# A Fourier-mixing and mixture-of-experts kernel on one core: the first expert layer of 512-row blocks in seven block products

## Chip, core and metric

The kernel runs on one core of one Trainium2 chip. The metric is the device time of one launch in microseconds (us); a time of the kernel before is the median of three launches. Profiles and traces are of one launch each, taken by the hardware profiler. The engines are called as the profile calls them: PE is TensorE (matmuls), PEld its weight loads, DVE is VectorE, ACT is ScalarE, POOL is GpSimd, SP is SyncE, which here issues most transfers.

## What is computed

The input is 8 batches of 2496 rows of 256 numbers. Each batch goes through a two-dimensional Fourier transform of which the real part is kept. Each of the 19,968 rows that result goes to the one of 8 experts whose gate value is the largest, and an expert is a network of two layers with 1024 numbers between them.

```python
X = np.fft.fft(np.fft.fft(x, axis=1), axis=2).real     # (8, 2496, 256)
x = X.reshape(19968, 256)
logits = x @ w_gate                                    # 8 experts
expert_idx = np.argmax(logits, axis=1)
gate_w = softmax(logits)[row, expert_idx]
for e in range(8):                                     # the rows of expert e
    h = np.maximum(x[rows_of_e] @ w1[e], 0.0)          # first layer, 256 to 1024
    y[rows_of_e] = h @ w2[e]                           # second layer, 1024 to 256
return gate_w[:, None] * y
```

All data are fp32. In the profile one fp32 matmul of the program shows as two MATMUL records and two LDWEIGHTS records; in the kernel it is one call of `mm`.

## The kernel before

The kernel works in rounds. While the rows of one batch go through the experts, the transform of the next batches is computed beside them. Rows are written by expert into `Xs` in device memory and come back as blocks of 512, 256 or 128 rows of one expert. The plan of the rounds is fixed: round 0 has two blocks of 256 rows and four of 128, round 1 four of 256, round 2 three of 512, rounds 3 to 6 five of 512 each, round 7 five of 512, then seven of 256 mixed with 21 of 128. That makes 28 blocks of 512 rows, 13 of 256 and 25 of 128.

The banks of PSUM, the memory that matmuls write, are shared out like this (a tile fills one of the eight banks or part of one):

```python
pm_ = ctx.enter_context(tc.tile_pool(name="pm_", bufs=3, space=PSUM))   # transform and routing
pst = ctx.enter_context(tc.tile_pool(name="pst", bufs=1, space=PSUM))   # transposes of a block
psh = ctx.enter_context(tc.tile_pool(name="psh", bufs=2, space=PSUM))   # first layer
psy = ctx.enter_context(tc.tile_pool(name="psy", bufs=2, space=PSUM))   # second layer
```

A block is transposed by `turn`, while the second layer of the block ahead of it runs:

```python
def turn(size, xb):
    xT = bp.tile([128, 2, BIG], F32, tag="xT", name="xT", bufs=1)
    n = min(size // 128, 2)
    for h in range(-(-size // 256)):
        pt = pst.tile([128, 2, n, 128], F32, tag="t", name="pt")
        for c in range(2):
            for t in range(n):
                nc.tensor.transpose(pt[:, c, t], xb[:, 2 * h + t, c * 128:(c + 1) * 128], ident[:])
        vec.tensor_scalar(xT[...], pt[...], con["alt"][:], None, op0=ALU.mult)
        yield xT
```

`experts` is a generator. Each `yield` of a number above zero says how much expert work was just issued, and gives the main loop the chance to issue steps of the transform before the next piece. With 512 rows `m` is 1, `FC` is 8 and `n` is 4, so that a block yields 8 times 1 and 4 times 2, 16 in all:

```python
for k, (b, size, last, at) in enumerate(todo):
    n, m = size // 128, BIG // size
    ...
    for f in range(FC // m):                                   # first layer
        ph = psh.tile([128, m, size], F32, tag="h", name="ph")
        for j in range(m):
            for c in range(2):
                mm(ph[:, j], w1_sb[:, c, (m*f+j)*128:(m*f+j+1)*128], xT[:, c, 0:size], c == 0, c == 1)
        o = hT[:, m * f:m * (f + 1), 0:size]
        if f % 2:
            vec.tensor_scalar(o, ph[:], 0.0, None, op0=ALU.max)
        else:
            act.activation(o, ph[:], ACTF.Relu)
        yield 1
    ...                                                        # turned = turn(the next block)
    for i in range(n):                                         # second layer
        xT = next(turned, xT)
        py = psy.tile([128, D], F32, tag="y", name="py")
        for f in range(FC):
            mm(py[:], hT[:, f, i * 128:(i + 1) * 128], w2_sb[:, f], f == 0, f == FC - 1)
        act.activation(y[:, i], py[:], ACTF.Copy, scale=xb[:, i, D + 1:D + 2])
        put_row(out, ro[:, i:i + 1], y[:, i], NT - 1, "out")   # indirect DMA, issued by POOL
        yield 2
```

The main loop spreads some 44 steps (`TICKS`) of the transform over the first 70% of a round's expert work; `side` is the generator of these steps:

```python
total = 16 * sum(k * size for size, k, _ in rounds()[b - 1]) / BIG
while done < total:
    w = next(work)
    done += w
    due += TICKS * w / (0.7 * total) if w else 1
    while due >= 1:
        next(side, None)
        due -= 1
for _ in side:
    pass
```

A step of the second stage of the transform holds, on PE, two matmuls of 120 columns into a tile `p` (copied by ACT to `zz`) and two of 145 and 146 columns into another `p`; from that ACT copies `zs` and DVE makes `lg` and two halves of `rows`. With every second such step goes a step of the first stage of the batch after: DVE folds `xq` (additions of 104 x 1024 and 104 x 508), PE makes two matmuls of 256 columns into `s`, ACT copies them to `t`. The steps of `route` are chains of small DVE operations up to `oh`, on which the matmuls into `rk` wait, and indirect writes of rows to `Xs` by POOL. All PSUM tiles of these steps come from the three buffers of `pm_`.

Of the kernel before, what the change touches and what calls it, by code (L numbers as in the profile page):

```python
# [34 lines left out]
E, F = 8, 1024  # L35
# [134 lines left out]


TICKS = 44
WARM = 16
MOST = max(k for now in rounds() for _, k, _ in now)

# [16 lines left out]
def kernel(ctx: ExitStack, tc, x, w_gate, w1, w2, out):  # L192
# [3 lines left out]
    def mm(o, lhsT, rhs, start=True, stop=True, **kw):  # L196
        nc.tensor.matmul(o, lhsT=lhsT, rhs=rhs, start=start, stop=stop, **kw)  # L197
# [305 lines left out]
    def turn(size, xb):  # L503

        xT = bp.tile([128, 2, BIG], F32, tag="xT", name="xT", bufs=1)
        n = min(size // 128, 2)
        for h in range(-(-size // 256)):
            pt = pst.tile([128, 2, n, 128], F32, tag="t", name="pt")
            for c in range(2):
                for t in range(n):  # L510
                    nc.tensor.transpose(pt[:, c, t], xb[:, 2 * h + t, c * 128:(c + 1) * 128], ident[:])  # L511
            vec.tensor_scalar(xT[:, :, 256 * h:256 * h + 128 * n], pt[:].rearrange("p c t k -> p c (t k)"),  # L512
                              con["alt"][:], None, op0=ALU.mult)
            yield xT

    def experts(todo):

        got, xT = [], None  # L520

        def fetch_some(k, most=3):

            while k + len(got) < len(todo) and len(got) < most and todo[k + len(got)][:3] in tabs:
                b, size, last, at = todo[k + len(got)]
                got.append(fetch(b, size, tabs[b, size, last], at))

        for k, (b, size, last, at) in enumerate(todo):
            n, m = size // 128, BIG // size
            if not k:  # L530
# [5 lines left out]
                for xT in turn(size, got[0][0]):  # L536
                    pass
            fetch_some(k)
            xb, w1_sb, w2_sb = got.pop(0)
            turned = iter(())  # L540
            follow = todo[k + 1] if k + 1 < len(todo) else None
            ro = bp.tile([128, BIG // 128], I32, tag="ro", name="ro", bufs=4)
            vec.tensor_copy(ro[:, 0:n], xb[:, 0:n, D])
            hT = bp.tile([128, FC, BIG], F32, tag="hT", name="hT", bufs=1)
            for f in range(FC // m):
                ph = psh.tile([128, m, size], F32, tag="h", name="ph")
                for j in range(m):
                    for c in range(2):
                        mm(ph[:, j], w1_sb[:, c, (m * f + j) * 128:(m * f + j + 1) * 128], xT[:, c, 0:size],
                           c == 0, c == 1)  # L550
# [6 lines that stand above are left out]
            if follow:  # L557
                while follow[:3] not in tabs:
                    yield 0
                fetch_some(k + 1, 2)  # L560
                turned = turn(follow[1], got[0][0])
# [61 lines left out]
    for _ in range(WARM):  # L623
        pw = psy.tile([128, D], F32, tag="y", name="py")
# [35 lines left out]
    for b in range(1, B):  # L660
# [66 lines left out]
```

## Time and profile before

| | before |
|---|---|
| three launches | 1398.54, 1403.64, 1409.75 us |
| profiled launch: span | 1367.9 us |
| PE busy | 1323.7 us, 97% of the span |
| PEld busy | 1007.3 us, 74% |
| DVE, ACT, POOL busy | 381.1, 284.2, 325.8 us |
| first layer, PE busy (tile `ph`) | 585.4 us, of it 396.7 us in the 512-column form |
| second layer, PE busy (tile `py`) | 580.8 us |
| granted TensorE clock, mean | 0.984 of full speed |

The span of the profiled launch is some 36 us less than the median of the three launches. The table of groups gives, for each kind of instruction, the sum of busy time, the mean duration of one, and after the second bar the idle time of its engine just before it with what ended that idle time. The records of matmuls overlap, so a mean duration times a count is more than the busy time; the pace of PE is read from the start times in the timeline.

### The profile page before, as it was taken

The numbers are of one execution on the slowest core, as the hardware profiler recorded it, in microseconds if no ns is written. First come the engines' busy times: TensorE is split into PE (matmuls) and PEld (weight loads), VectorE is DVE, ScalarE is ACT, GpSimd is POOL, SyncE is SP. The second block draws the span as 40 slices with busy tenths as digits, with TensorE's granted clock in tenths as the row PEclk, the third lists the DMA queues.
The fourth block names the chain that finished last, engine by engine and source line by source line (L and its number), as shares of the span: only waits on it lengthen the run. The fifth ranks groups of instructions, "written<-read, shape, count | busy, mean of one in ns | idle before, by whom it ended". The sixth has DMA issues, their size and how long they took to land.

```text
span 1367.9 us, 17145 instructions
## 1 busy us (share of the span) xinstructions
PE 1323.7 (97%) x6190; PEld 1007.3 (74%) x6190; DVE 381.1 (28%) x1182; ACT 284.2 (21%) x656; POOL 325.8 (24%) x335
## 2 busy tenths in 40 slices
PE   5769999999999999999999999999999999999998
PEld 3659987776766667767767767666776689999997
DVE  4643334431333224222233212224111111111111
ACT  1422131321222113211222112221111111111111
POOL 0335144143032211331122411331311111111111
PEclk8779999999999999999999999999999999999999
DMA  8769876455364424534234242414323327777772
GB/s 251 248 243 344 325 242 243 160 161 203 132 203 159 182 106 143 159 137 171 95 138 169 92 156 99 173 65 173 127 97 120 131 92 273 278 283 282 275 264 102
DMA packets 63089, 249.50 MB, mean 182 GB/s; under 512 B 10057, under 2 KB 24883, under 8 KB 43420
## 3 DMA queue, kind: packets, MB, share of 16 engines
q1 hardware_dynamic: 46231, 203.33, 42.0%
q0 software_dynamic: 15888, 42.14, 8.5%
q10 hardware_dynamic: 885, 2.94, 0.6%
q8 instruction: 49, 0.80, 0.2%
q14 instruction: 36, 0.29, 0.1%
HBM read 194.97 MB, written 54.83 MB: 183 GB/s over the span
## 4 chain that ended last, share of the span: by engine, by line
PE 53%; issue 31%; POOL 7%; DMA 2%; DVE 1%; POOLq 0%; ACT 0%; SPq 0%; ACTq 0%; DVEq 0%
PE py L197 23%; PE ph L197 22%; POOL out_dram L212 5%; PE p L197 4%; PE s L197 2%; POOL Xs L212 2%; PE pt L511 2%; DMA Xs<-rows,pi 1%; DMA xb<-Xs 1%; DMA Xs<-pad,ti 0%; DMA w_sb<-in_moe_w_dram 0%; POOLq L212 0%; PE rk L197 0%; DVE hT L553 0%; DVE rows L389 0%
## 5 line engine op out<-in xcount | busy, mean ns | idle before, releaser
L197 PE MATMUL ph<-xT,w_sb 128*128 128x512 f32 (+2 forms) x2112 | 585.4, 431 | 1.9 <-DMA w_sb<-in_moe_w_dram 1.9
L197 PE MATMUL py<-w_sb,hT 128*128 128x256 f32 x2608 | 580.8, 379 | 0.0
L197 PEld LDWEIGHTS py<-w_sb,hT 128*128 128x128 f32 x2608 | 487.3, 190 | 62.0
L197 PEld LDWEIGHTS ph<-xT,w_sb 128*128 128x128 f32 x2112 | 339.7, 191 | 196.5 <-issue 177.4
L212 POOL DMA_INDIRECT out_dram<-y,ro x163 | 159.1, 976 | 864.8 <-ACT y L568 846.5
L553 DVE TENSOR_SCALAR hT<-ph 128x512 f32<-128x512 f32 x163 | 112.7, 692 | 688.8 <-PE ph L197 344.7
L568 ACT ACTIVATE y<-py,xb 128x256 f32<-128x256 f32 x163 | 77.3, 474 | 602.6 <-PE py L197 602.6
L212 POOL DMA_INDIRECT Xs<-rows,pi x160 | 158.7, 992 | 172.0 <-issue 73.3
L555 ACT ACTIVATE hT<-ph 128x512 f32<-128x512 f32 x163 | 97.3, 597 | 326.8 <-PE ph L197 326.8
L512 DVE TENSOR_SCALAR xT<-pt,table 128x512 f32<-128x512 f32 (+1 forms) x94 | 63.3, 674 | 71.0 <-PE pt L511 71.0
L197 PE MATMUL s<-xq,w 104*112 104x256 f32 (+2 forms) x208 | 59.5, 409 | 12.8 <-DVE xq L276 12.6
L197 PEld LDWEIGHTS p<-table,t 120*128 120x128 f32 x352 | 54.7, 204 | 18.5 <-issue 12.0
L387 DVE COPY lg<-p 128x16 f32<-128x16 f32 x80 | 13.9, 174 | 181.6 <-ACT zs L384 181.4
L511 PE MATMUL pt<-table,xb 128*128 128x128 f32 x326 | 51.9, 275 | 8.7 <-DMA xb<-Xs 8.7
L511 PEld LDWEIGHTS pt<-table,xb 128*128 128x128 f32 x326 | 40.5, 142 | 25.3 <-issue 11.6
L197 PE MATMUL p<-table,t 120*128 120x120 f32 (+1 forms) x352 | 57.0, 289 | 1.7 <-DVE rows L389 1.4
L197 PE MATMUL p<-table,zz 128*128 128x145 f32 (+1 forms) x320 | 56.2, 300 | 2.6 <-DVE rows L389 1.4
L197 PEld LDWEIGHTS s<-xq,w 104*112 104x112 f32 x208 | 38.3, 198 | 25.0 <-DVE xq L276 9.3
L197 PEld LDWEIGHTS p<-table,zz 128*128 128x128 f32 x320 | 45.9, 196 | 6.2 <-issue 2.4
L389 DVE SCALAR_TENSOR_TENSOR rows<-p,zs 128x129 f32<-128x129 f32 x160 | 48.2, 343 | 1.4 <-issue 0.2
L300 ACT COPY t<-s 112x512 f32<-112x512 f32 x48 | 27.9, 584 | 52.2 <-PE s L197 43.6
L358 ACT COPY zz<-p 128x240 f32<-128x240 f32 (+1 forms) x88 | 31.0, 352 | 35.0 <-PE p L197 34.6
(81 smaller groups left out, 303.2 us busy)
## 6 DMA issues: line engine op xcount, KB each, us to landing
w_sb<-in_moe_w_dram SPq DMA_DIRECT2D x132, 1024.0 KB, 7.4
xq<-in_x_dram SPq DMA_DIRECT2D x24, 896.0 KB, 9.7
xb<-Xs SPq DMA_DIRECT2D x28, 516.0 KB, 3.8
Td<-t SPq DMA_DIRECT2D x18, 448.0 KB, 3.3
t<-Td SPq DMA_DIRECT2D x8, 768.0 KB, 5.4
t<-Td SPq DMA_DIRECT2D x8, 640.0 KB, 6.4
xb<-Xs SPq DMA_DIRECT2D x13, 258.0 KB, 3.2
xb<-Xs SPq DMA_DIRECT2D x25, 129.0 KB, 2.5
```

The source lines that it names most:

```text
L197: nc.tensor.matmul(o, lhsT=lhsT, rhs=rhs, start=start, stop=stop, **kw)
L212: return unordered(pool.indirect_dma_start(out=dst, out_offset=bass.IndirectOffsetOnAxis(ap=idx, axis=0), in_=rows, in_offset=None, bounds ...
L300: act.copy(t1[:, 2 * half:2 * half + 2], ps[:])
L358: act.copy(zz[:, :, g * GP:g * GP + n], p2[:])
L387: vec.tensor_copy(lg[:, k:k + 2], p3[:, NY:NY + 2 * E].rearrange("p (m e) -> p m e", m=2))
L389: vec.scalar_tensor_tensor(rows[:, k + m, 0:NY], p3[:, 0:NY], zs[:, 0:1], zs[:, 1:], op0=ALU.add, op1=op)
L511: nc.tensor.transpose(pt[:, c, t], xb[:, 2 * h + t, c * 128:(c + 1) * 128], ident[:])
L512: vec.tensor_scalar(xT[:, :, 256 * h:256 * h + 128 * n], pt[:].rearrange("p c t k -> p c (t k)"), con["alt"][:], None, op0=ALU.mult)
L553: vec.tensor_scalar(o, ph[:], 0.0, None, op0=ALU.max)
L555: act.activation(o, ph[:], ACTF.Relu)
L568: act.activation(y[:, i], py[:], ACTF.Copy, scale=xb[:, i, D + 1:D + 2])
```

## The change

The aim is to spend fewer matmul columns on the first layer of the 28 blocks of 512 rows. A product of two matrices that are each cut into two by two parts takes eight products of parts when done plainly. It can be done with seven, with some sums and differences of parts ahead of the products and others behind them (the form of Strassen and Winograd). Here w1 of an expert is cut into two halves of its 256 inputs (`c`) and two halves of its 1024 outputs, the rows of a block into two halves of 256.

- `left`, four additions or subtractions of 128 x 512 on POOL, makes the combinations of the parts of w1; three go to a new buffer `ws`, one back into `w1_sb`.
- `right`, four of 128 x 256 on DVE, does the same for the parts of the transposed block; three go to `xs`, one back into `xT`. Both belong to `turn` now, so they are issued beside the second layer of the block ahead.
- `seven` does the products, with a moving operand of 256 columns instead of 512, in two groups of seven. They go to five PSUM banks, `a` to `e`; a bank is reused in the group as soon as its first content was read. DVE and ACT add up the parts and apply the ReLU on the way to `hT`.
- The four pools `pst`, `psh` and `psy` become one pool `pse` of these five banks, of which the transposes use `e`, the plain first layer `a` and `c`, the second layer `b` and `d`. `pm_` keeps its three.
- `seven` has no `yield`: no step of the transform is issued within the first layer of such a block. The second layer yields twice per 128 rows instead of once, so the sum per block stays 16. The 0.7 of the main loop becomes 0.6.

Blocks of 256 and 128 rows keep the plain first layer.

```diff
+HALVED = (512,)
...
-    pst = ctx.enter_context(tc.tile_pool(name="pst", bufs=1, space=PSUM))
-    psh = ctx.enter_context(tc.tile_pool(name="psh", bufs=2, space=PSUM))
-    psy = ctx.enter_context(tc.tile_pool(name="psy", bufs=2, space=PSUM))
+    pse = ctx.enter_context(tc.tile_pool(name="pse", bufs=1, space=PSUM))
...
+    def left(eng, o, a11, a12, a21, a22):
+        eng.tensor_tensor(o[0], a21, a22, op=add)
+        eng.tensor_tensor(o[1], o[0], a11, op=sub)
+        eng.tensor_tensor(a21, a11, a21, op=sub)
+        eng.tensor_tensor(o[2], a12, o[1], op=sub)
+        return a11, a12, o[2], a22, o[0], o[1], a21
...                                      # right: four of the same kind on b11, b12, b21, b22
     def turn(size, got):
+        if size in HALVED:
+            ws = bp.tile([128, 3, F // 2], F32, tag="ws", name="ws", bufs=1)
+            f = F // 2
+            l = left(pool, [ws[:, k] for k in range(3)],
+                     *(w1_sb[:, c, k * f:(k + 1) * f] for k in range(2) for c in range(2)))
...                                      # transposes and xT as before, pt in bank "e"
+        if size in HALVED:
+            th = size // 2
+            xs = bp.tile([128, 3, th], F32, tag="xs", name="xs", bufs=1)
+            r = right(vec, [xs[:, k] for k in range(3)],
+                      *(xT[:, c, k * th:(k + 1) * th] for c in range(2) for k in range(2)))
+            yield l, r
+    def seven(size, l, r, hT):
+        th = size // 2
+        fp = 512 // th
+        half = FC // 2
+        def product(g, k, o, fresh=True):
+            for j in range(fp):
+                f = g * fp + j
+                mm(o[:, j], l[k][:, f * 128:(f + 1) * 128], r[k], fresh and not j, j == fp - 1, skip_group_check=True)
+        for g in range(half // fp):
+            a, b, c, d, e = (pse.tile([128, fp, th], F32, tag=k, name=k) for k in "abcde")
...                                      # p1, u2, u3 in SBUF; h11 to h22 are parts of hT
+            product(g, 0, a)
+            act.copy(p1[:], a[:])
+            product(g, 5, b)
+            vec.tensor_tensor(u2[:], p1[:], b[:], op=add)
+            product(g, 6, d)
+            vec.tensor_tensor(u3[:], u2[:], d[:], op=add)
+            product(g, 4, c)
+            vec.tensor_tensor(h22, u3[:], c[:], op=add)
+            product(g, 1, a, False)
+            act.activation(h11, a[:], ACTF.Relu)
+            act.activation(h22, h22, ACTF.Relu)
+            product(g, 3, e)
+            vec.tensor_tensor(h21, u3[:], e[:], op=add)
+            act.activation(h21, h21, ACTF.Relu)
+            product(g, 2, c, False)
+            vec.tensor_tensor(h12, u2[:], c[:], op=add)
+            act.activation(h12, h12, ACTF.Relu)
...
-            for f in range(FC // m):
-                ph = psh.tile([128, m, size], F32, tag="h", name="ph")
+            if size in HALVED:
+                seven(size, *xT, hT)
+            for f in range(FC // m if size not in HALVED else 0):
+                ph = pse.tile([128, m, size], F32, tag="ac"[f % 2], name="ph")
...
-                py = psy.tile([128, D], F32, tag="y", name="py")
+                py = pse.tile([128, D], F32, tag="bd"[i % 2], name="py")
                 for f in range(FC):
                     mm(py[:], hT[:, f, i * 128:(i + 1) * 128], w2_sb[:, f], f == 0, f == FC - 1)
+                    if f == FC // 2 - 1 and size in HALVED:
+                        yield 2
...
-            due += TICKS * w / (0.7 * total) if w else 1
+            due += TICKS * w / (0.6 * total) if w else 1
```

More of the change, by code (lines that the diff above doesn't have):

```diff
@@ L501, in fetch, with right, turn @@
         return xb, w1_sb, w2_sb
-    def turn(size, xb):
+    add, sub = ALU.add, ALU.subtract
+    def left(eng, o, a11, a12, a21, a22):
[4 more added lines that the diff above has]
+        return a11, a12, o[2], a22, o[0], o[1], a21
+    def right(eng, o, b11, b12, b21, b22):
+        eng.tensor_tensor(o[0], b12, b11, op=sub)
+        eng.tensor_tensor(o[1], b22, o[0], op=sub)
+        eng.tensor_tensor(b12, b22, b12, op=sub)
+        eng.tensor_tensor(o[2], b21, o[1], op=sub)
+        return b11, b21, b22, o[2], o[0], o[1], b12
+    def turn(size, got):
+        xb, w1_sb, _ = got
         xT = bp.tile([128, 2, BIG], F32, tag="xT", name="xT", bufs=1)
         n = min(size // 128, 2)
+        if size in HALVED:
[3 more added lines that the diff above has]
+                     *(w1_sb[:, c, k * f:(k + 1) * f] for k in range(2) for c in range(2)))
         for h in range(-(-size // 256)):
-            pt = pst.tile([128, 2, n, 128], F32, tag="t", name="pt")
+            pt = pse.tile([128, 2, n, 128], F32, tag="e", name="pt")
             for c in range(2):
@@ L514, in turn @@
             yield xT
+        if size in HALVED:
[14 more added lines that the diff above has]
+            a, b, c, d, e = (pse.tile([128, fp, th], F32, tag=k, name=k) for k in "abcde")
+            p1, u2, u3 = (bp.tile([128, fp, th], F32, tag=n, name=n, bufs=1) for n in ("p1", "u2", "u3"))
+            h11, h12, h21, h22 = (hT[:, k * half + g * fp:k * half + (g + 1) * fp, t * th:(t + 1) * th]
+                                  for k in range(2) for t in range(2))
+            product(g, 0, a)
[15 more added lines that the diff above has]
+            act.activation(h12, h12, ACTF.Relu)
     def experts(todo):
@@ L535, in experts @@
                     yield 0
-                for xT in turn(size, got[0][0]):
+                for xT in turn(size, got[0]):
                     pass
@@ L560, in experts @@
                 fetch_some(k + 1, 2)
-                turned = turn(follow[1], got[0][0])
+                turned = turn(follow[1], got[0])
             y = bp.tile([128, BIG // 128, D], F32, tag="y", name="y", bufs=3)
@@ L622 @@
     nc.sync.dma_start(out=wg[:], in_=w_gate)
-    for _ in range(WARM):
-        pw = psy.tile([128, D], F32, tag="y", name="py")
+    for k in range(WARM):
+        pw = pse.tile([128, D], F32, tag="bd"[k % 2], name="py")
         mm(pw[:], ones[:], bc(ones[:], 1, 2))
```

## The prediction, made before the changed kernel ran

> **What bounds the kernel now.** I read the page's busy shares and slices first, then the groups by form, the waits of PE, the timeline of PE where no step of the transform is left, and busy time by round.
>
> ```profile
> PE 1323.7 (97%) x6190; PEld 1007.3 (74%) x6190; DVE 381.1 (28%) x1182; ACT 284.2 (21%) x656; POOL 325.8 (24%) x335
> ...
> PE   5769999999999999999999999999999999999998
> ```
>
> PE is busy 97% of the span, and all that it lacks lies in the first three slices (some 100 us of start-up). No other engine passes 28%. Busy time alone does not prove that PE is at its limit, so the pace comes from the start times of a run of pure expert blocks:
>
> ```profile
> 998.68 13.90 PE L197 MATMUL ph<-xT,w_sb 128*128 128x512 f32 x32
> 1012.41 0.60 PE L511 MATMUL pt<-table,xb 128*128 128x128 f32 x4
> 1012.85 3.62 PE L197 MATMUL py<-w_sb,hT 128*128 128x256 f32 x16
> 1016.31 0.60 PE L511 MATMUL pt<-table,xb 128*128 128x128 f32 x4
> 1016.75 10.53 PE L197 MATMUL py<-w_sb,hT 128*128 128x256 f32 x48
> 1027.11 13.90 PE L197 MATMUL ph<-xT,w_sb 128*128 128x512 f32 x32
> ```
>
> Columns: start, length, what. One block takes 1027.11 - 998.68 = 28.43 us. The first layer is 1012.41 - 998.68 = 13.73 us for 16 fp32 matmuls of 512 columns: 0.858 us each, 1.676 ns per column. The second is 10.36 us (1016.75 to 1027.11) for 24 matmuls of 256 columns: 0.4317 us each, 1.686 ns per column. So half as many columns per weight load costs only 0.6% more per column. Nothing stands between the groups: this is PE's own pace.
>
> Beside the transform it is the same:
>
> ```profile
> 385.36:544.45 159.09, 159.09 (x661) 110.81 (x661) 45.38 (x135) 34.83 (x81) 39.00 (x40) 1.00 0.43 151
> 544.45:703.54 159.09, 159.09 (x661) 110.81 (x661) 45.39 (x135) 34.76 (x81) 39.01 (x40) 1.00 0.42 145
> ```
>
> Two rounds of five blocks (columns: stretch, length, then busy us of PE, PEld, DVE, ACT, POOL; last granted clock, DMA share, GB/s). Five pure blocks would be 142.15 us, which leaves 16.9 us for a round's steps. Their PE work, counted from the kernel, is some 2560 columns of 120 or 80, 2910 of 145 and 146, and 3328 of the first stage: 8800 x 1.68 = 14.8 us, with 1 to 2 us of small matmuls. So the steps wait for practically nothing. The few waits of PE in the whole launch:
>
> ```profile
> PE s L197 <- DVE xq L276: 12.6, 3, 5.1
> PE pt L511 <- DMA xb<-Xs: 8.7, 3, 7.0
> PE pr L197 <- DMA t<-Td: 5.0, 2, 3.8
> PE rk L197 <- DVE oh L410: 4.9, 4, 2.6
> ```
>
> (us in total, times, longest; most of it at the start.) Conclusion: columns of PE set the time; what takes columns away is gained, unless it makes PE wait.
>
> **What the Trainium skill says.** "TensorE: Matmul & The Clock Gate", Part 2, step-by-step: weight loads are pulled ahead of running matmuls and overlap them. The trace agrees: the loads of `py` take 190 ns each, the matmuls of `py` follow each other every 216 ns (half of 0.4317 us) with 0.0 us idle. "GPSIMD Engine Reference", 3.1: a two-input elementwise operation costs about 2.6 cycles per element there, 4497 ns measured for 2048 fp32 elements; a quarter of it, 1.1 us for 128 x 512, is my estimate for one operation of `left`. No run here has one yet. "SBUF — State Buffer", Who interferes with whom: a DVE instruction with two SBUF inputs and a GpSimd instruction that reads SBUF exclude each other for the whole instruction. That would bear on `left` against the folds of the transform and `right`; the trace of before has no elementwise work on POOL and cannot show it.
>
> **The change, part by part.**
>
> 1. First layer of a 512-row block. Away: 16 matmuls of 512 columns, 13.73 us. In: 2 groups x 7 products x 2 matmuls = 28 matmuls of 256 columns, the very form of `py`: 28 x 0.4317 = 12.09 us. Saved 1.64 us per block, times 28 blocks = **46 us**, 3.4% of the profiled span.
>
> 2. Adding up inside `seven`. A product is two matmuls, 0.86 us. Per group of 6.04 us DVE has five additions of 128 x 512, from 0.69 us each by the ReLU row (692 ns for the same shape out of PSUM): 3.5 us. ACT has a copy and four ReLUs at 0.6 us (597 ns): 3.0 us. Both fit. I follow the banks from the group's start at 0: `a` is full at 0.86 and needed again at 3.45; its copy ends near 1.7. `c` is full at 3.45 and needed at 5.2; DVE has read it by about 4.3. The next group takes `a` at 6.04, read by 5.1. So each bank comes free about a microsecond early. The second layer needs the parts of the last-but-one product only at its seventh matmul, some 3 us later. Cost on PE: about 0.
>
> 3. `left`: 4 x 1.1 = 4.5 us of POOL per block (126 us in all, POOL 326 to about 450 of 1330). Its first result is needed one second layer later (over 14 us), and the weights were fetched a block earlier. Hidden, but it can hold DVE folds for up to 1 us apiece.
>
> 4. `right`: 4 x about 0.36 us of DVE (between 242 ns for 80 and 681 ns for 508 elements), issued before the third row group of the second layer, so over 6 us ahead. Hidden.
>
> 5. The steps move. In a five-block round 44 steps / (0.6 x 80) = 0.92 per unit of work, and the second layer alone carries them: 1.83 after each half row group of 4 matmuls (1.73 us). Before it was 0.79 per 1.72 us of first layer. Steps in pairs are closer to each other than their chains: PE to ACT to DVE and back over three `pm_` buffers, DVE 0.17 + 2 x 0.34 = 0.86 us per step plus folds. Rounds 0 and 1 already run 44 / (0.7 x 32) = 1.96 per unit, and there the trace shows one wait of 0.9 us and 0.3 us of smaller ones. Walking through the changed order of a five-block round I find three places: the first `pr` and `p` (0.3 us), one `s` behind `rows` (0.7 us), and the first `rk`, which comes two steps behind the last `rows` (1 to 2 us). I take **2 us per round, four rounds: 8 us**. The three-block round has 3.06 steps per half row group: **3 us**. Tighter steps in rounds 0 and 1: 1 us, against 1.6 us of a wait for `xb` (near 229 us) that an earlier end of the steps may take away. Sum: about 10 to 12 us, with the scatter of POOL against DVE in it.
>
> 6. Round 7's 28 small blocks (at half and a quarter of 28.43 us for 256 and 128 rows: 7 x 14.2 + 21 x 7.1 = some 250 us), the start and the transfers' bytes stay as they are.
>
> Net: 46 - 10 = 36 us. That is 2.6% of the profiled span; from 1403.6 us I come to **1368 us**.
>
> **Rivals.** (a) *The steps, squeezed into half the time, make PE wait.* For: every step is a chain through three engines and three buffers, and `rk` waits on a chain of seven DVE operations. Against: steps three in a row (around 175 us) cost the kernel before only some 0.4 us in waits. If it holds, 5 us per round and more: a gain of 15 to 20 us, 1385 us, within 2%. (b) *POOL or DVE becomes the bound of the first layer*: `left` much slower than estimated, or queued behind indirect writes that wait for rows. For: POOL works in order, and each `put_row` waits for another engine. Against: no steps lie in the first layer, so POOL's queue is empty when `left` starts. It would cost 2 to 5 us per block, 55 us and more, and the change would be slower: 1410 us or above. (c) *All is hidden*: 46 us and the `xb` wait, 1356 us.
>
> **Range and chances.** From all hidden (46 to 48 us, and launch-to-launch scatter of 5 us: 1351) to rival (a) at its worst (1392). Faster by over 2% needs 28 us, waits of under 18 us; I give that 0.70. Within 2%: 0.27, nearly all rival (a). Slower: 0.03, rival (b).
>
> **What the profile after would show.** Products into `a` to `e` with 28 x 0.43 us per block and blocks 26.8 us apart at the start of round 7: step 1 right. Idle of PE on DVE or ACT inside `seven`: step 2 wrong. A PE wait for POOL (`ws`), or operations of `left` above 3 us: step 3 wrong. Rounds of five blocks should fall from 159.1 to about 153 us (159.1 - 8.2 + 2); if they stay above 156, step 5 is wrong, and `rk`, `s` or `p` in PE's waits will say where. The prediction would also fail if matmuls that take turns between banks and weights keep a slower pace than `py` does.

## The result, and the profile after

| | before | after |
|---|---|---|
| median of four launches each, one session | 1401.29 us | 1467.34 us |
| ratio after/before, 95% interval | | 1.0461 [1.0412, 1.0509] |
| profiled launch: span | 1367.9 us | 1465.1 us |
| mean granted TensorE clock | 0.984 | 0.951 |

The change makes the kernel 4.6% slower; the prediction had 2.6% faster. From the page of the changed kernel, the busy shares and two rows of the slices:

```profile
PE 1332.3 (91%) x6862; PEld 1161.3 (79%) x6862; DVE 578.7 (39%) x1462; ACT 380.7 (26%) x824; POOL 477.2 (33%) x447
...
PE   5687989987998799988998989988998999999998
...
PEclk8779998999999999989999999999999999999999
```

The row of PE was nines before, from the fourth slice to the last but one; now it has sevens and eights up to the end of the transform. It has unbroken nines only in the last quarter, where no step runs beside the experts. No other engine passes 39%, so what appeared is waiting, not a new bound.

The products themselves do what they were to do. PE's timeline of the changed kernel (start, length, what) for the last block of round 6, beside which no step of the transform is left; round 7 starts at 1067.93:

```profile
1041.01 1.03 PE L198 MATMUL a<-xT,w_sb 128*128 128x256 f32 x4
1041.88 1.03 PE L198 MATMUL b<-xs,ws 128*128 128x256 f32 x4
...
1053.68 3.62 PE L198 MATMUL py<-w_sb,hT 128*128 128x256 f32 x16
...
1067.93 1.03 PE L198 MATMUL a<-xT,w_sb 128*128 128x256 f32 x4
```

From block to block 1067.93 - 1041.01 = 26.92 us, where before it was 28.43: 1.51 us saved. A product takes 1041.88 - 1041.01 = 0.87 us, and there is no gap between the fourteen.

Where the transform runs beside them it is otherwise. Three rounds of five blocks, before and then after (columns as in the prediction: stretch, length, busy us of PE, PEld, DVE, ACT, POOL, clock, DMA share, GB/s):

```profile
339.84:817.24 477.40, 477.30 (x1981) 332.51 (x1980) 136.13 (x402) 104.45 (x244) 117.00 (x120) 1.00 0.41 145
```

```profile
385.94:904.50 518.56, 475.20 (x2341) 410.38 (x2340) 250.23 (x552) 156.54 (x333) 199.45 (x180) 0.96 0.37 134
```

The ideal for a round is 159.1 less five times the expected 1.64 us, 150.9 us. The changed kernel takes 518.56 / 3 = 172.9 us. PE is idle for (518.56 - 475.20) / 3 = 14.5 us of it and busy for 158.4 us, 7.5 us more than the ideal. Of this excess, 4.8 us are the clock: it is at one half for 37.6 us of the three rounds, PE is busy for 28.5 of them, and half of that is lost. Another 0.7 us is gain that did not come (1.51 instead of 1.64 us a block); the other 2 us are not explained here. The waits of PE in the whole launch (us, times, longest):

```profile
PE c L198 <- DVE hT L571: 29.5, 7, 6.8
PE rk L198 <- DVE oh L409: 21.6, 15, 2.8
PE p L198 <- ACT zz L357: 19.7, 11, 6.2
PE p L198 <- issue: 17.9, 8, 4.0
```

The first is inside `seven`: bank `c` is to be written a second time and DVE has not read it. The other three are transform steps. Seven waits of up to 6.8 us are not what a slightly tight bank would give. The timeline of one of them, in the fourth block of round 6, PE, ACT, DVE and POOL together (in brackets: idle time before, and what ended it):

```profile
1006.29 1.03 PE L198 MATMUL a<-xT,w_sb 128*128 128x256 f32 x4
...
1008.28 0.97 POOL L213 DMA_INDIRECT Xs<-rows,pi  x1 [0.31 <-issue]
...
1009.61 0.58 ACT L565 COPY p<-a 128x512 f32<-128x512 f32 x1 [2.42 <-PE d L198]
...
1012.48 0.69 DVE L567 TENSOR_TENSOR u<-p,b 128x512 f32<-128x512 f32 x1 [11.62 <-PE e L198]
1013.39 0.97 POOL L213 DMA_INDIRECT out_dram<-y,ro  x1 [0.31 <-issue]
1015.25 0.69 DVE L569 TENSOR_TENSOR u<-u,d 128x512 f32<-128x512 f32 x1 [2.08 <-remote]
1016.68 0.69 DVE L571 TENSOR_TENSOR hT<-u,c 128x512 f32<-128x512 f32 x1 [0.75 <-remote]
...
1017.52 1.97 PE L198 MATMUL c<-xT,ws 128*128 128x256 f32 x4 [5.27 <-DVE hT L571]
```

`a` is complete at 1007.3. ACT has nothing else to do, yet its copy starts at 1009.61. DVE has been idle for 11.62 us and starts its first addition 2.3 us after that copy has ended, and the next two 2.8 and 1.4 us later, although `d` and `c` are full by 1009.9. All that while POOL issues indirect writes back to back, nine of them, 1.28 us apart, from 1003.17 to 1013.39 (two are shown, the others cut). The increments by which PE tells that it is done are recorded at 1006.69, 1009.53, 1012.39 and 1015.22, then three within 0.12 us; the starts of ACT at 1009.61 and of DVE at 1012.48 and 1015.25 follow one of these by 0.03 to 0.09 us. So the engines are not slow; **they learn late that their input is there**. I call these late signals.

After the wait comes a second cost. Two stretches of the same place, with the columns as above, show the clock at 0.50 for 3.4 us:

```profile
1006.00:1017.00 11.00, 5.90 (x27) 4.53 (x25) 1.69 (x3) 1.26 (x3) 6.53 (x7) 1.00 0.26 91
1017.60:1021.00 3.40, 3.40 (x9) 2.69 (x10) 1.05 (x2) 1.66 (x3) 0.00 (x0) 0.50 0.00 0
```

The same happens to a transform step in the second layer of the changed kernel:

```profile
454.48 0.68 PE L198 MATMUL p<-table,t 120*128 120x120 f32 x4 [0.16 <-issue]
455.38 0.97 POOL L213 DMA_INDIRECT Xs<-rows,pi  x1 [0.31 <-issue]
456.66 0.97 POOL L213 DMA_INDIRECT out_dram<-y,ro  x1 [0.30 <-issue]
457.94 0.97 POOL L213 DMA_INDIRECT Xs<-rows,pi  x1 [0.31 <-issue]
460.92 0.36 ACT L357 COPY zz<-p 128x240 f32<-128x240 f32 x1 [7.60 <-remote]
...
461.33 1.34 PE L198 MATMUL p<-table,zz 128*128 128x145 f32 x4 [6.17 <-ACT zz L357]
```

ACT idles 7.60 us; the matmuls for its copy were done 5.8 us earlier. PE waits 6.17 us and then needs 1.34 us for four records that take 0.67 at full clock.

### The profile page after: what moved, and what is told of

It reads as the page before. It is cut to its first block, busy times and chain, and to the rows that moved or that the text cites. A ratio compares the mean times of both kernels' runs of the same rounds, so it can differ in the third digit from the quotient of the medians.

```text
span 1465.1 us, 19369 instructions
## 1 busy us (share of the span) xinstructions
PE 1332.3 (91%) x6862; PEld 1161.3 (79%) x6862; DVE 578.7 (39%) x1462; ACT 380.7 (26%) x824; POOL 477.2 (33%) x447
## 4 chain that ended last, share of the span: by engine, by line
PE 60%; issue 21%; DVE 5%; POOL 4%; another core or an unknown queue 3%; ACT 1%; DMA 1%; POOLq 0%; DVEq 0%; ACTq 0%
PE py L198 25%; PE a L198 7%; PE c L198 7%; PE p L198 5%; PE b L198 3%; PE d L198 3%; PE e L198 3%; PE ph L198 3%; POOL out_dram L213 3%; PE pt L535 2%; PE s L198 2%; POOL Xs L213 1%; DMA Xs<-rows,pi 1%; DVE eq L403 1%
## 5 line engine op out<-in xcount | busy, mean ns | idle before, releaser
L213 POOL DMA_INDIRECT Xs<-rows,pi x160 | 159.0, 994 | 149.2 <-DVE rows L388 53.2
L198 PE MATMUL ph<-xT,w_sb 128*128 128x128 f32 (+1 forms) x1216 | 190.3, 313 | 2.3 <-issue 1.3
L198 PEld LDWEIGHTS ph<-xT,w_sb 128*128 128x128 f32 x1216 | 173.2, 193 | 15.8 <-issue 2.4
L621 DVE TENSOR_SCALAR hT<-ph 128x512 f32<-128x512 f32 x51 | 35.3, 691 | 288.3 <-issue 209.8
L506 POOL TENSOR_TENSOR ws<-w_sb 128x512 f32<-128x512 f32 x28 | 35.6, 1271 | 315.7 <-issue 289.9
L567 DVE TENSOR_TENSOR u<-p,b 128x512 f32<-128x512 f32 x56 | 38.5, 688 | 223.7 <-PE b L198 109.1
L198 PE MATMUL a<-xT,w_sb 128*128 128x256 f32 x448 | 121.5, 395 | 3.1 <-issue 1.8
L198 PEld LDWEIGHTS a<-xT,w_sb 128*128 128x128 f32 x448 | 87.8, 198 | 18.0 <-issue 3.4
L198 PE MATMUL c<-xT,ws 128*128 128x256 f32 x224 | 63.0, 407 | 29.5 <-DVE hT L571 29.5
L573 ACT ACTIVATE hT<-a 128x512 f32<-128x512 f32 x56 | 33.4, 597 | 176.0 <-PE a L198 135.3
L198 PEld LDWEIGHTS c<-xT,ws 128*128 128x128 f32 x224 | 44.7, 203 | 38.5 <-issue 32.1
```

The costliest lines, as they stand in the source:

```text
L213: return unordered(pool.indirect_dma_start(out=dst, out_offset=bass.IndirectOffsetOnAxis(ap=idx, axis=0), in_=rows, in_offset=None, bounds ...
L506: eng.tensor_tensor(o[0], a21, a22, op=add)
L567: vec.tensor_tensor(u2[:], p1[:], b[:], op=add)
L573: act.activation(h11, a[:], ACTF.Relu)
```

## The experiments

The theories. **S**: the steps, squeezed beside the second layer only, cost the time by their own chains. **H**: late signals cost it, and the five banks of `seven`, each used again within a few matmuls, feel them most. **L**: `left` on POOL holds up DVE. **P**: late signals belong to the changed kernel only. Each run is compared with launches of the kernel before that were made beside it on the same chip; late signals were there in most sessions and absent in one, where the kernel before takes 1371 us instead of 1391 to 1403. The profiled launch of before was one without them too.

This table shows the three five-block rounds together, one third of each sum; the excess is busy time over 150.9 us with products and over 159.1 without.

| kernel | round, us | PE idle | excess busy |
|---|---|---|---|
| before, with or without late signals | 159.1 | 0.0 | 0 |
| after | 172.9 | 14.5 | 7.5 |
| left_dve | 172.9 | 14.5 | 7.5 |
| steps (squeeze, plain first layer) | 170.1 | 6.8 | 4.1 |
| spread (products, steps spread) | 162.2 | 7.4 | 3.9 |
| d_before (fewer indirect writes) | 160.0 | 0.7 | 0.2 |
| d_after | 162.6 | 7.8 | 3.9 |
| d_spread | 160.5 | 6.4 | 3.2 |
| p_after (writes to `Xs` one at a time) | 160.6 | 6.9 | 2.8 |
| p_spread | 157.7 | 4.8 | 2.1 |
| best, late signals (r_best) | 157.1 | 4.7 | 1.6 |
| best, without (v_best) | 155.1 | 3.0 | 1.2 |

**The kernel before, once more.** No edit.

> The kernel before, run once more with a trace. In the trace of the changed kernel the semaphore increments of PE, DVE and ACT arrive up to 7 us (PE) late while POOL issues indirect writes in a row; in the first trace of before (1367.9 us) all of PE's arrive within 14 ns. Theory H, held signals (something holds back the engines' increments while POOL makes its indirect writes, in some launches, whatever the kernel): the other launches of before take about 1400 us because of it, so this trace has late increments too and a span near 1400 us. Rival P (the lateness belongs to the changed program alone): none here, and the 30 us between 1370 and 1400 us are something else.

Measured: 1392.27 us, ratio 0.9989 [0.9975, 1.0002]; profiled 1388.7 us. This launch has late signals: an eviction of `y`, which follows the last matmul of `py` by 0.04 us otherwise, comes up to 4.8 us after it. Its waits of PE:

```profile
PE s L197 <- DVE xq L276: 11.0, 3, 5.7
PE p L197 <- ACT zz L358: 10.5, 8, 3.9
```

The wait of `p` for `zz` was 0.8 us in the first launch. All that is lost lies in rounds 0 to 2, which grow by 20.8 us (339.8 to 360.6); the rounds of five stay at 159.1. P falls in part: the kernel before meets late signals too, but in this launch only in rounds 0 to 2. In the rounds of five none of the 120 evictions of `ph` starts over 0.04 us after its matmuls and its engine's work ahead of it are done, though POOL issues up to 13 indirect writes in a row there. So it does not show that the kernel before has slack for late signals; it has none to meet there. (At least 57 of PE's 909 increments have no record in this trace, some of them where the reader starts at once, so lateness is read here from the starts.) Against this launch the changed one loses 25.3 us in rounds 0 to 2, 41.2 in rounds 3 to 5, 10.4 in round 6 and gains 0.5 in round 7: together 76 us.

**Products, with the steps spread as before.** `seven` yields eight times 1, spread over its fourteen products, the second layer once per 128 rows, and 0.7 is back.

```diff
-                seven(size, *xT, hT)
+                yield from seven(size, *xT, hT)        # 8 times 1 in all
...
-                    if f == FC // 2 - 1 and size in HALVED:
-                        yield 2
...
-            due += TICKS * w / (0.6 * total) if w else 1
+            due += TICKS * w / (0.7 * total) if w else 1
```

> The changed kernel, but with the steps of the transform spread as before: the first layer yields 8 times within its 14 products, the second once per row group, and 0.7 in place of 0.6. Theory S (the squeezed steps make PE wait): the waits on oh, zz and rows go away and the time falls below before, to 1350 to 1375 us. Theory H (held signals together with the tight reuse of five banks): the waits of the products for DVE and ACT stay, since indirect writes now fall into the first layer as well; 1430 us or more.

Measured: 1408.02 us, 1.0119 [1.0083, 1.0154]. Of the loss of 4.6% in after, 1.2% is left, so the placing of the steps matters; but the products still cost 15 us where they should save 46. It is neither the 1350 to 1375 us of S alone nor the 1430 and more of H alone. Waits of PE:

```profile
PE p L198 <- ACT zz L357: 9.7, 7, 4.5
PE pt L535 <- DVE xT L536: 9.6, 7, 1.5
PE c L198 <- DVE hT L583: 8.6, 8, 3.0
PE a L198 <- ACT hT L587: 7.7, 4, 2.3
```

Banks `c` and `a` of `seven` and the transposes in `e` wait without any squeeze. S alone is not enough.

**Steps squeezed, plain first layer.** The complement: no products, no `left`, no `right`; the five banks, the 0.6 and the steps beside the second layer only stay.

```diff
-HALVED = (512,)
+HALVED = ()
+BESIDE = (512,)
...
-                yield 1
+                if size not in BESIDE:
+                    yield 1
...
-                    if f == FC // 2 - 1 and size in HALVED:
+                    if f == FC // 2 - 1 and size in BESIDE:
```

> The plain first layer of before in the changed kernel's pools (five banks), with the steps of the transform beside the second layer only and 0.6: no products, no combinations, nothing new on POOL. Theory S: this alone costs most of the 46 us saved and the 66 us lost, so 1470 us or more against 1401 of before. Theory H with tight banks: the plain first layer has 1.7 us per bank and two banks in turn, so it loses little: 1405 to 1425 us.

Measured: 1447.35 us, 1.0375 [1.0344, 1.0407]: 54 us lost without a single product. The five banks are not it: with the same plain layer in them and the steps spread over 0.7 (the nine-block run below), rounds 0 to 2 take 84.0, 82.6 and 107.4 us, in the launch of before above 82.0, 82.4 and 107.3. Waits of PE:

```profile
PE rk L199 <- DVE oh L410: 15.2, 11, 2.8
PE p L199 <- issue: 13.0, 9, 2.4
PE s L199 <- DVE xq L276: 12.4, 3, 5.2
PE p L199 <- ACT zz L358: 10.7, 8, 3.1
```

H put it at 1405 to 1425 and S at 1470 or more; it fell between, nearer to S. By round: the squeeze costs 11.0 us in each round of five, 12.6 in round 6, 13.7 in rounds 0 and 1 together (170.9 + 82.4 to 180.1 + 86.9), which hold no block of 512 rows and feel only the 0.6 and the banks (with 0.7 and the same banks, in the spread form, they end at 255.3 instead of 267.0, so it is mostly the 0.6). It costs 0.9 in round 2. The steady rounds add up: 11.0 for the squeeze, 162.2 - 150.9 = 11.3 for the products with spread steps, together 22.3, against 172.9 - 150.9 = 22.0 in the changed kernel. Two faults of like size, then, though not independent ones, as the thinned writes below show. Round 2 (107.3 us in the launch of before above) is the exception: 117.3 with products and spread steps, 119.3 after, so there the products are nearly all of the loss.

**`left` on DVE.**

```diff
-            l = left(pool, [ws[:, k] for k in range(3)],
+            l = left(vec, [ws[:, k] for k in range(3)],
```

> The changed kernel with the four combinations of w1 on DVE in place of POOL, about 4 x 0.69 us of DVE per block. Theory L (elementwise work on POOL disturbs: it shuts DVE out, which in the trace stretches an operation of 0.24 us to 1.2 to 1.3 us, and it delays POOL's writes): 1400 us or less. Theories H and S: POOL's indirect writes and the place of the steps are the same, so within 20 us of the changed kernel's 1467 us.

Measured: 1462.43 us, 1.0486 [1.0459, 1.0513]; its rounds of five are those of after. L falls as the cause. The mutual hold-up it rests on is real, as the timeline of the changed kernel shows:

```profile
480.38 0.22 DVE L402 TENSOR_REDUCE mx<-lg 128x10 f32<-128x80 f32 x1
480.57 1.26 POOL L507 TENSOR_TENSOR ws<-ws,w_sb 128x512 f32<-128x512 f32 x1
480.63 1.29 DVE L403 TENSOR_TENSOR eq<-lg,mx 128x80 f32<-128x80 f32 x1
481.79 1.27 POOL L508 TENSOR_TENSOR w_sb<-w_sb 128x512 f32<-128x512 f32 x1
481.96 1.19 DVE L404 TENSOR_TENSOR eq<-eq,table 128x80 f32<-128x80 f32 x1
```

`eq` takes 0.24 us elsewhere and 1.29 here, until POOL's operation is over: what the Trainium skill, "SBUF — State Buffer", Who interferes with whom, says of a DVE instruction with two inputs in SBUF beside a GpSimd instruction that reads SBUF. It delays one chain to `rk` per round by 2 us, and four DVE additions in its place cost as much.

**Fewer indirect writes.** The result rows leave by plain transfers in the order of the blocks, not by indirect writes to their places, so the output is not in the reference's order. POOL keeps only the writes to `Xs`.

```diff
-                put_row(out, ro[:, i:i + 1], y[:, i], NT - 1, "out")
+                nc.sync.dma_start(out=out[r:r + 128], in_=y[:, i])     # r: next 128 rows
```

> The kernel before with half of POOL's indirect writes taken away: each 128 rows of the result go out by a plain transfer from SP in the order of the blocks, not to their own rows, so the output is not the reference's; everything else is the same. Theory H (the engines' signals are held while POOL makes indirect writes in a row): far fewer late increments, and the 20 us between the two traces of before (1367.9 and 1388.7 us) come back in good part: 1370 to 1382 us. Rival R (lateness comes with the transfers on the DMA queues, whoever issues them): late increments and about 1390 us as before.

> The same for the changed kernel: only the result's rows leave by plain transfers in block order (not the reference's output). Theory H: the late increments fall to less than half, with them the waits of the products for DVE (30 us) and of p for zz, and the half-clock time behind them: 1400 to 1425 us. Rival S alone (chains of the squeezed steps, with no part of POOL's writes in it): 1455 us or more.

> The same for the products with the steps spread as before. Theory H says that the products lose their gain to held signals and little else: 1340 to 1360 us, 20 us or more under the kernel before with the same plain transfers. If the products' own handoffs over five banks are too tight even without held signals, it stays at 1385 us or more.

Measured: before so edited 1393.12 us, 0.9963 [0.9947, 0.9978]; after 1408.7, 1.0056 [1.0037, 1.0075]; the spread form 1395.95, 0.997 [0.9955, 0.9985]. The transfers themselves bring the kernel before 6 us; they bring the changed kernel some 58 (1467.34 to 1408.7, across sessions; by ratio 4 points). With the steps as squeezed as ever, 10.2 us of each round of five are gone. Waits of PE in the changed kernel so edited:

```profile
PE rk L198 <- DVE oh L409: 21.7, 15, 2.9
PE c L198 <- DVE hT L571: 15.3, 6, 5.0
PE p L198 <- ACT zz L357: 11.0, 5, 3.7
```

`c` and `zz` halve, which is H. `rk` stays (21.6 to 21.7 us): that is the bare chain of DVE operations, which is S. Two expectations of H were missed. The spread form did not come to 1340 to 1360 us: writes to `Xs` are still issued up to 10 in a row. And the kernel before did not come to 1370 to 1382 us, as rival R of its expectation had it: its late signals did not go away. Twelve of its 163 evictions of `y` start over 0.5 us late with ACT free, against three in c_before, and its rounds of five grow to 160.0 us. R itself, that any transfer brings lateness, does not fit where they lie: all twelve have five of POOL's writes in the 6 us ahead of them, as 16 evictions have, and of the other 147 none is late. In all profiled launches but v_best and the first of before, 338 evictions have four or five such writes ahead of them, and 121 of these are late; of the other 2596 none is.

**Writes to `Xs` one at a time.** From the second batch on, the indirect writes of rows are put in a list and given to POOL one at a time beside the expert work, instead of in a row behind their step; the plan of the next round waits until the list is empty. The result's writes are indirect again. They were meant to be some 3 us apart, but POOL takes them in order with the result's writes: half of them still start 1.28 us after the one ahead. What falls is the longest run of writes in the rounds of five, from 13 to 8 in the changed kernel and to 6 in the spread form.

```diff
-            sent(put_row(Xs, pi[:, s:s + 1], rows[:, s], E * CAP - 1, "xs"), b)
+            later.append((pi[:, s:s + 1], rows[:, s], b))    # one leaves per total / 54 of work
+            if not b:
+                put_one()
```

> The kernel before with the same indirect writes, but those to Xs spaced: the 20 of a batch wait in a list and go out one at a time beside the expert work, some 3 us apart, in place of one after every step; steps of the transform unchanged, the plan of the next round waits until the list is empty. Theory H: late increments of PE nearly vanish outside the start, and the time falls to 1370 to 1382 us. If lateness needs only many writes, not writes in a row: no change, 1393 us.

> The changed kernel (steps beside the second layer only, 0.6) with the writes to Xs spaced. Theory H with S: waits of products for DVE go from 30 to under 8 us, waits of rk for oh (22 us, the chain of the squeezed steps) stay; 1390 to 1420 us against 1467.

> Seven products in all 28 blocks, steps spread as before, and the writes to Xs spaced in the same way. Theory H: without held signals the products keep most of their gain of 1.5 us per block, so 25 us or more below the spaced kernel before: 1335 to 1360 us. If the five banks are too tight by themselves, or the chains of seven products and steps meet on DVE: within 10 us of the spaced kernel before.

Measured: before so edited 1413.68 us, 1.0066 [1.0039, 1.0093]; after 1433.25, 1.0206 [1.0171, 1.0241]; spread 1409.6, 1.0058 [1.0039, 1.0077]. All three miss what H expected of the whole time, and spread is within 10 us of before, as its rival had it. The rounds of five are the ones to read. After falls from 172.9 to 160.6 with its steps and products where they were, spread from 162.2 to 157.7, before stays at 159.1. The whole time hides it, for a new wait, by the waits of PE in the changed kernel so edited:

```profile
PE pt L544 <- DMA xb<-Xs: 30.7, 3, 11.7
PE rk L198 <- DVE oh L416: 24.4, 15, 4.2
PE c L198 <- DVE hT L580: 14.8, 6, 4.1
```

At the ends of rounds 0 to 2 the next blocks wait for rows that were held back. `c` falls to 14.8 us, not under the 8 that were expected. Two ways of thinning POOL's writes thus give back 10 to 12 us per round, as much as spreading the steps. They overlap with it: with both (p_spread) it is 15.1. Put the other way, the squeeze costs 10.7 us per round with the writes as they were (172.9 against 162.2), but 2.1 with fewer writes (162.6 against 160.5) and 2.9 with the writes to `Xs` one at a time (160.6 against 157.7). PE's waits of `rk` for `oh` in these rounds are 8.6 us in after, d_after and p_after, 2.9 per round (1.3 in steps), and none in spread. So in the changed kernel 2 to 3 us of the squeeze are its own chains, and most of the rest comes by way of the writes.

**Products only where no step runs.** Nine blocks: the fifth of rounds 3 to 6 and the five of round 7, with 0.7 and everything else plain, in the five banks.

```diff
-HALVED = (512,)
+def quiet(b, size, last, at):
+    return size == 512 and (b == B - 1 or b > 2 and at == 4)
...
```

> Seven products only in blocks with no step of the transform beside their first layer: the fifth block of rounds 3 to 6 and the five of round 7, nine of 28; steps spread as before, 0.7. In the trace of the changed kernel such a block takes 26.92 us against 28.43 us. If the products are sound by themselves: 9 x 1.5 = 13 us less than before, 1380 us. If they lose even there (combinations on POOL, tight banks): 1393 us or more.

Measured: 1393.74 us, 0.9959 [0.9943, 0.9974]: 5 us gained instead of about 13. Round 7's five blocks take 135.7 instead of 141.7 us, but the rounds of five stay at 159.0: each has about 1 us of waits of `ph` for DVE, and at 988 us, in round 6, `pt` waits 4.8 us for `xT`. Even there, new waits take some of it back.

**Both mended.** Products in the 25 blocks of rounds 3 to 7, steps spread with 0.7, writes to `Xs` one at a time only beside rounds of five (`if b < 4: put_one()` issues the earlier ones at once), so that the wait for `xb` does not come.

```diff
-HALVED = (512,)
+def halved(b, size, last, at):
+    return size == 512 and b > 2
...
-                seven(size, *xT, hT)
+                yield from seven(size, *xT, hT)
...
+            later.append((pi[:, s:s + 1], rows[:, s], b))
+            if b < 4:
+                put_one()
```

> Seven products in the 25 blocks of rounds 3 to 7 alone, steps spread as before (0.7), writes to Xs spaced only beside the rounds of five blocks (in the spaced runs the three waits for xb of 9 to 12 us stood at the ends of the short rounds 0 to 2). By rounds, from the runs so far: 171 + 82 + 107 for rounds 0 to 2, as in the second trace of before, 157 each for rounds 3 to 5, 151.6 for round 6, 136 for round 7, 251.5 and 4 for the rest: some 1375 us in that trace's state, about 1% below before. If the spacing costs waits for xb here too, or the products lose in the rounds with steps: 1390 us or more, no better than before.

Measured, in a session without late signals: 1347.19 us against 1371.23, ratio 0.9819 [0.9804, 0.9833]. Its three rounds of five:

```profile
341.88:807.14 465.26, 456.31 (x2341) 400.05 (x2340) 231.21 (x552) 155.16 (x334) 195.06 (x180) 1.00 0.42 149
```

155.1 us per round, with the clock at 1.00: 4.2 us above the ideal, of which 3.0 idle. Nearly all of this idle time is two waits for DVE, `pt` for `xT` (4.5 us in the three rounds) and `c` for `su` (3.6 us).

**The main kernels on other chips.** No edit: `r_` are after, spread, steps and best once more on another chip, `s_` after and steps in a further session, meant to catch one without late signals.

> The changed kernel unchanged, together with the next three, so that all four stand against the same runs of before. In the last runs the kernel before took 1371 us and no increment came late (largest lag 14 ns); in the three sets ahead of it, on two other chips, it took 1393 to 1403 us and increments came up to 7 us late. If the lateness is a property of the chip: before near 1371 us here means no lateness, and then the prediction's sum should hold, apart from the waits of the squeezed steps: theory S by itself gives 150.9 + about 5 us per round of five, 1365 to 1385 us; before near 1400 us means lateness, and again 1460 to 1470 us.

> Products in all 28 blocks, steps spread as before. If no lateness: 4 to 5 us gained per round of five and 7 us in round 7, 1340 to 1352 us; with lateness 1408 us again.

> The plain first layer with the steps beside the second layer only. If no lateness, what is lost is the chains of the squeezed steps alone: 3 to 6 us per round of five, 1390 to 1400 us against 1371 of before; with lateness 1447 us again.

> Products in the 25 blocks of rounds 3 to 7, steps spread, writes to Xs spaced beside rounds of five. If no lateness 1347 us again, 1.8% under before; with lateness 1375 to 1385 us, 1 to 1.5% under before.

> The changed kernel once more, to meet a chip on which before takes about 1371 us and no increment comes late. If it does: 1365 to 1385 us if the squeezed chains cost what the prediction gave them or up to twice that; above 1400 us if the chains alone undo the gain. If before takes about 1395 us: 1460 us again.

> The plain first layer with the steps beside the second layer only, beside it. With no lateness: 1380 to 1400 us, the chains alone. With lateness: 1447 us again.

| | us | ratio, interval |
|---|---|---|
| r_after | 1457.42 | 1.0459 [1.0414, 1.0504] |
| r_spread | 1408.4 | 1.0108 [1.0066, 1.015] |
| r_steps | 1448.16 | 1.0405 [1.0357, 1.0452] |
| r_best | 1378.02 | 0.9888 [0.9848, 0.9929] |
| s_after | 1456.4 | 1.0465 [1.0445, 1.0486] |
| s_steps | 1444.63 | 1.0394 [1.0362, 1.0427] |

The order holds everywhere, the rounds of five are within 2 us of those in the table, and the mended kernel beats the kernel before with late signals (by 1.1%) and without (by 1.8%). Both new sessions had late signals (evictions of `y` up to 5.6 us late in both `s_` launches), so the changed kernel was never seen without them.

## Why the prediction was wrong

**Step 1 held**: 1.51 instead of 1.64 us per block, 42 instead of 46 us for 28 blocks.

**Step 2 failed**: "each bank comes free about a microsecond early", "Cost on PE: about 0". The walk through the banks is right where nothing else runs (no gap in the last block of round 6), but it gave ACT and DVE their start at the moment PE was done. With late signals that start comes up to 6 us later, and a microsecond of slack is nothing. It happens without any step as well: in round 7, at 1100 us, `c` waits 4.2 us while POOL writes padding rows to `Xs`. PE's waits for DVE on bank `c` make 33.2 us in the changed kernel (29.5 and 3.7), plus the half clock behind them. With spread steps the products cost 11.3 us per round of five above the ideal; 4.2 remain without late signals and with the writes to `Xs` one at a time. So some 60% of this term went when both did, and the rest is mostly waits for DVE that the prediction also held at zero.

**Step 3** was off in size and right in effect. An operation of `left` took 1.27 to 1.40 us in the mean instead of 1.1, and holds DVE up by about 1 us as said; moved to DVE, it changed nothing that helps.

**Step 4 held**: `right` took 0.42 to 0.44 us per operation instead of 0.36, and does not appear among PE's waits.

**Step 5 failed, and is the largest miss**: "2 us per round, four rounds: 8 us", "3 us", "1 us". With a plain first layer the squeeze measured 11.0 us per round of five (9.0 and 10.9 in the two later launches), 12.6 in round 6, 13.7 in rounds 0 and 1: 60 us in profiled launches (33.0 + 12.6 + 0.9 + 13.7), not 12. The prediction's own test said that rounds above 156 us would mean this, and that `rk`, `s` or `p` would say where; `rk` and `p` do. For the chains alone its 2 us per round were about right: that much, 2.1 to 2.9 us, is left of the squeeze once POOL's writes are thinned. What it lacked is that the squeeze brings POOL's writes closer together too (two runs of 11 to 13 in each round of five, where the kernel before has one), and that signals come late beside them. It read the small waits of rounds 0 and 1 as proof that steps three in a row are cheap, from the one launch of before without late signals. The sign was on the page: a span of 1367.9 us beside launches of 1399 to 1410. The gap was noted, and the launch's lack of waits carried over to the others all the same.

**A term that was not in the sum**: the clock. In the changed kernel, waits of 2.6 to 6.8 us are followed by 3.4, 6.8 or 10.2 us at half clock. The mean clock fell from 0.984 to 0.951. From 100 us to PE's last matmul the changed kernel has 92.2 us at half speed, the first launch of before none; PE is busy for 71.6 of them, and half of that, 36 us, is lost. With PE's idle time over the same stretch, 93.2 against 3.3 us, the sum is 90 + 36 - 42 = 84 us, and the profiled spans differ by 97.2; the other 13 us are not explained here. The Trainium skill, "TensorE: Matmul & The Clock Gate", Part 1, What's actually happening, puts the slow clock after an idle window of about 3.4 us. The length agrees: all stretches are multiples of 3.41 us. That PE must be idle for all of it does not. Cut into the clock record's steps of 3.41 us, the twenty traces show, after their first 100 us, half clock after every step at full clock in which PE idles for over 1.97 us in sum, and after none with under 1.76 us. So a wait of 2 us can already bring 3.4 us at half clock, a surcharge of 1.7 us.

**Rivals.** (a) had squeezed steps that make PE wait, at 5 us per round and more, about half of what was measured, but not the late signals. (b) named 1410 us and above for another reason, `left`, and that reason falls. (c) is out.

**What stays open.** The changed kernel and the squeeze were never met without late signals, so the 2 to 3 us per round of five that its own chains cost are known only from the thinned writes, and with products only. Why signals come late while POOL issues indirect writes in a row, and why in some sessions only, no run shows. Such a run is not enough: the kernel before has runs of 13 in its rounds of five and no late start there, the spread form has the same runs and starts up to 5.6 us late. What is shown is that every late eviction of `y` has four or five such writes in the 6 us ahead of it, and that in the changed kernel fewer or more scattered writes shorten the waits.

## What to carry to other kernels

A bank that comes free a microsecond early on paper is only as safe as the signal that says so: here starts came up to 6 us late, and a change that saves matmuls by using banks sooner had no room for it. Before steps are packed closer, look what else then comes in a row, here POOL's indirect writes, and spread or thin it first. And if the profiled launch is shorter than the timed ones, find out what it did not meet before its lack of waits is taken as proof.

## What the hardware showed unexpectedly

- While POOL issued indirect writes back to back (1.28 us apart), ACT and DVE started up to 6 us after PE had finished their input, and PE's increments were recorded 2.84 us apart and then in a burst. Ten of 163 evictions of `y` in the changed kernel came over 0.5 us late with ACT free, the worst 5.7 us; in the launch of before without late signals, none came later than 0.04 us.
- The same program has sessions with and without this: the kernel before takes 1371 us in one and 1391 to 1403 in the others. A chip with the same number, 15, had both.
- PE's clock was halved after every 3.41 us step of its record in which PE had idled for over 1.97 us in sum, not only after steps without work.
- A two-input DVE operation of 128 x 80 takes 0.24 us alone and up to 1.30 while POOL runs a two-input operation of 128 x 512.
